# A chunked state-space scan before a squared-ReLU feed-forward layer: 64-token chunks on 32x32 array tiles

## The chip, the cores and the metric

The kernel runs on one core of a Trainium2 chip. A core has five engines with queues of their own: TensorE (PE; its weight loads are shown as PEld), VectorE (DVE), ScalarE (ACT), GpSimd (POOL) and SyncE (SP, here only a DMA queue). The metric is the device time of one execution in microseconds, and lower is better. A profile is of one execution; its clock starts at its first instruction.

## The reference

Inputs are x (4 x 8 x 768 x 32), a (4 x 8 x 768), B and C (4 x 8 x 768 x 16) and the two weights of the feed-forward layer, w_in (256 x 2048) and w_out (2048 x 256). Cut to what matters, and with the batch and the head left out:

```python
log_a = np.log(np.clip(a, 1e-06, 1.0))
for c in range(S // 32):                       # chunks of 32 tokens
    cum = np.cumsum(log_a[sl])
    L = np.exp(cum[:, None] - cum[None, :]) * causal
    y[sl] = ((Cc @ Bc.T) * L) @ xc + (Cc @ state) * np.exp(cum)[:, None]
    state = np.exp(cum[-1]) * state + (Bc * np.exp(cum[-1] - cum)[:, None]).T @ xc
out = np.maximum(y_all @ w_in, 0) ** 2 @ w_out     # y_all: 3072 tokens x 256 (8 heads x 32)
```

The size of the chunk doesn't change the result: a longer one moves work from the state to the product inside the chunk. N = 16 is the size of a state, D = 32 that of a head.

## The kernel before

The 3072 tokens are cut into 12 blocks of 256 (a batch and a third of its sequence; `PAIRS`, L107). Each block goes through the scan, which yields T, and then through the feed-forward layer in eight pairs of 128-wide slices.

The feed-forward layer sets the beat. There are 96 steps (L385), one for each block and pair of slices. In step s, `mm1` (L296) issues four 128x128 products with 256 columns into a PSUM tile hps (two buffers), ACT applies the ReLU (L305), DVE squares the result of the step before (L311), and `mm2` (L314) issues four products of the step `LAG` = 4 earlier into ops. After a block's last slice ACT copies ops to osb (L326), and SP stores it (L327).

Between these, the scan of a coming block is issued in small parts. A block is two chunks (u) of 128 tokens, each with 64 even and 64 odd tokens (r). For block k, with s0 = 8k - 12, the dictionary `todo` of the loop at L405 holds:

- s0 - 12: `ph_load` of C, B and x on SP (L118);
- s0 - 4: `ph_prep` on POOL: C times the running product of a into cz (L142), B cast into Bb (L156), x divided by the running product into xs (L162);
- s0: `ph_tr`, six transposes on TensorE (L181, L183) into PSUM, and DVE's copy to bct (L185);
- s0 + 1: `ph_u`, 16 products of B and x (L224, array tiles of 64 rows x 32 columns), and DVE's state updates (L237 to L241);
- s0 + 2: `ph_mt`, 16 products of B and C with 256 columns (L195, tiles of 32 x 64), then four masks on DVE (L206);
- s0 + 6: `ph_y`, 16 products with the state (L264, tiles of 32 x 32 on the diagonal) and 32 with the masked matrix (L276, tiles of 64 x 32), and ACT's copy to T (L290).

All four share one PSUM tile of four banks (`ps_s`, tag A), one after the other. Each engine runs its instructions in the order written (`manual_schedule`), and semaphores hold an instruction until what it reads is written and what it writes is free. Blocks 0 and 1 are scanned ahead of the loop. The weights come in five pairs of DMAs, the first pair on ACT's queue and the rest on SP's, between the loads of blocks 0 to 3; ACT casts w_in (L133) and POOL w_out (L134).

Of the kernel before, what the change touches and what calls it, by code (L numbers as in the profile page):

```python
# [10 lines left out]
FP32 = mybir.dt.float32  # L11
BF16 = mybir.dt.bfloat16
# [18 lines left out]
def kernel(  # L31
# [16 lines left out]
    NPAIR = 12  # L48
    LAG = 4
    LEAD = 12  # L50
# [6 lines left out]
    big = ctx.enter_context(tc.tile_pool(name="big", bufs=2))  # L57
# [10 lines left out]
    tok = 2 * np.arange(64)[None, :] + np.arange(2)[:, None]  # L68
    later = tok.reshape(-1)
    mask_np = np.zeros((128, 2, 128), np.float32)  # L70
    for u in range(2):
        for r in range(2):
            mask_np[64 * u:64 * u + 64, r, :] = (tok[r][:, None] <= later[None, :])
# [6 lines left out]
    cb_np = np.concatenate([np.eye(128, dtype=np.float32), mask_np.reshape(128, 256)],  # L80
                           axis=1).astype(ml_dtypes.bfloat16)
# [18 lines left out]
    cz = [const.tile([128, 2, 240], BF16, name=f"cz{i}") for i in range(3)]  # L100
# [6 lines left out]
    PAIRS = [(b, j) for j in range(3) for b in range(4)]  # L107


    loaded = {}  # L110

    def ph_load(k, order="CBx", eng=None):
        b, j = PAIRS[k]
        t = {}
        for what in order:
            src, w = {"B": (B, N), "C": (C, N), "x": (x, D)}[what]
            dst = nat.tile([128, NH, 2 * w], FP32, tag=f"{what}_nat", name=f"{what}_nat{k}")
            (eng or nc.sync).dma_start(  # L118
                out=dst, in_=_dap(src, (b * NH * S + j * 256) * w,
                                  [[2 * w, 128], [S * w, NH], [1, 2 * w]]))  # L120
            t[what] = dst
        loaded[k] = t
# [13 lines left out]

    live = {}

    def prep_c(k, eng):
        b, j = PAIRS[k]  # L140
        czk = cz[k % 3]
        eng.tensor_tensor(  # L142
            out=_fap(czk, 0, [[240, 2], [32, 8], [1, 16]]),
            in0=_fap(loaded[k]["C"], 0, [[16, 2], [32, 8], [1, 16]]),
            in1=_fap(P_sb, b * 24 + j, [[96, 2], [3, 8], [0, 16]]), op=ALU.mult)
        live.setdefault(k, {})["cz"] = czk

    def prep_b(k, eng):
        Bb = prep.tile([128, 2, 128], BF16, tag="Bb", name=f"Bb{k}")
        for r in range(2):  # L150
            bo = _fap(Bb, r * 128, [[16, 2], [32, 4], [1, 16]])
            bi = _fap(loaded[k]["B"], r * 16, [[128, 2], [32, 4], [1, 16]])
            if eng is nc.scalar:
                eng.copy(out=bo, in_=bi)  # L154
            else:
                eng.tensor_copy(out=bo, in_=bi)  # L156
        live.setdefault(k, {})["Bb"] = Bb

    def prep_x(k, eng):
        b, j = PAIRS[k]  # L160
# [7 lines left out]
    def ph_prep(k):  # L168
        prep_c(k, nc.gpsimd)
        prep_b(k, nc.gpsimd)  # L170
        prep_x(k, nc.gpsimd)
# [3 lines left out]
    def ph_tr(k):  # L175
        v = live[k]
        pool, tag = (ps_o, "ops") if k < 2 else (ps_s, "A")
        tr = pool.tile([128, 2, 3, 128], BF16, tag=tag, name=f"tr{k}",
                       padded_shape=[128, 2, 4, 128] if k < 2 else [128, 8, 4, 128])
        for r in range(2):  # L180
            nc.tensor.transpose(tr[:, r, 0, :], v["Bb"][:, r, :], eye_b)  # L181
            for g in range(2):
                nc.tensor.transpose(tr[:, r, 1 + g, :], v["cz"][:, r, 112 * g:112 * g + 128], eye_b)  # L183
        bct = big.tile([128, 2, 3, 128], BF16, tag="bct", name=f"bct{k}")
        nc.vector.tensor_copy(out=bct, in_=tr)  # L185
        v["bct"] = bct

    def ph_mt(k):
        v = live[k]
        bct = v["bct"]  # L190
        mt = ps_s.tile([128, 4, 2, 2, 128], FP32, tag="A", name=f"mt{k}")
        for u in range(2):
            for r in range(2):
                for q in range(4):
                    nc.tensor.matmul(  # L195
                        mt[64 * u:64 * u + 64, q, r, :, :],
                        bct[32 * q:32 * q + 32, r, 0, u * 64:u * 64 + 64],
                        _fap(bct[32 * q:32 * q + 32], 128 + u * 64, [[128, 2], [384, 2], [1, 64]]),
                        start=True, stop=True, skip_group_check=True,
                        tile_position=(32 * q, 64 * u))  # L200
        v["mt"] = mt
        v["mts"] = big.tile([128, 4, 2, 2, 128], BF16, tag="mts", name=f"mts{k}")

    def ph_mask(k, q):
        v = live[k]
        nc.vector.tensor_tensor(  # L206
            out=v["mts"][:, q], in0=v["mt"][:, q],
            in1=_fap(cb, 128, [[128, 2], [0, 2], [1, 128]]), op=ALU.mult)

    def ph_u(k):  # L210
        b, j = PAIRS[k]
        v = live[k]
        if k < 2:
            U = [ps_h.tile([128, 64], FP32, tag="hps", name=f"U{k}_{u}", padded_shape=[128, 512])
                 for u in range(2)]
        else:
            t = ps_s.tile([128, 4, 512], FP32, tag="A", name=f"U{k}")
            U = [t[:, u, 0:64] for u in range(2)]
        for r in range(2):
            for u in range(2):  # L220
                if j == 2 and u == 1:
                    continue
                for q in range(4):
                    nc.tensor.matmul(  # L224
                        U[u][32 * q:32 * q + 32, :],
                        v["Bb"][64 * u:64 * u + 64, r, 32 * q:32 * q + 32],
                        _fap(v["xs"][64 * u:64 * u + 64], r * 256 + q * 32, [[128, 2], [1, 32]]),
                        start=(r == 0), stop=(r == 1), skip_group_check=True,
                        tile_position=(64 * u, 32 * q))
        S_u = [state.get(b)]  # L230
        for u in range(2):
            if j == 2 and u == 1:
                break
            ptot = Ptot[:, u, b * 3 + j:b * 3 + j + 1]
            S_n = spool.tile([128, 64], BF16, tag=f"S{b}{u}", name=f"S{k}_{u}")
            if S_u[u] is None:
                nc.vector.tensor_scalar(out=S_n, in0=U[u], scalar1=ptot, scalar2=None, op0=ALU.mult)  # L237
            else:
                z = spool.tile([128, 64], FP32, tag="z", name=f"z{k}_{u}")
                nc.vector.tensor_tensor(out=z, in0=U[u], in1=S_u[u], op=ALU.add)  # L240
                nc.vector.tensor_scalar(out=S_n, in0=z, scalar1=ptot, scalar2=None, op0=ALU.mult)  # L241
            S_u.append(S_n)
        v["S"] = S_u
        state[b] = S_u[-1]
# [3 lines left out]
    def ph_y(k):  # L248
        b, j = PAIRS[k]
        v = live.pop(k)  # L250
        if k < 2:
            Y = [ps_h.tile([128, 2, 128], FP32, tag="hps", name=f"Y{k}_{u}", padded_shape=[128, 4, 128])
                 for u in range(2)]
        else:
            t = ps_s.tile([128, 4, 4, 128], FP32, tag="A", name=f"Y{k}")
            Y = [t[:, u, 0:2, :] for u in range(2)]
        first = {(u, q): True for u in range(2) for q in range(4)}
        for u in range(2):
            S_b = v["S"][u]
            if S_b is None:  # L260
                continue
            for g in range(2):
                for q in range(4):
                    nc.tensor.matmul(  # L264
                        Y[u][32 * q:32 * q + 32, g, :],
                        S_b[32 * q:32 * q + 32, g * 32:(g + 1) * 32],
                        _fap(v["bct"][32 * q:32 * q + 32], 128 + g * 128 + u * 64, [[384, 2], [1, 64]]),
                        start=first[(u, q)], stop=False, skip_group_check=True,
                        tile_position=(32 * q, 32 * q))
                    first[(u, q)] = False  # L270
        for g in range(2):
            for r in range(2):
                for u in range(2):
                    for q in range(4):
                        h = 4 * g + q
                        nc.tensor.matmul(  # L276
                            Y[u][32 * q:32 * q + 32, g, :],
                            v["xs"][64 * u:64 * u + 64, r, h * 32:h * 32 + 32],
                            v["mts"][64 * u:64 * u + 64, q, r, g, :],
                            start=first[(u, q)], stop=(g == 1 and r == 1), skip_group_check=True,  # L280
                            tile_position=(64 * u, 32 * q))
                        first[(u, q)] = False

# [160 lines left out]
```

## Time and profile before

| what | value |
|---|---|
| median of 3 runs | 131.57 us (131.39 to 131.71) |
| span of the profiled execution | 129.5 us |
| own time of the profiled execution | the page gives none beside the span; 2.0 us lie between it and the median |
| busy: TensorE, DVE, ACT, POOL | 86%, 70%, 58%, 24% |
| mean granted TensorE clock | 0.997 |
| large products mm1, mm2 (L301, L321) | 384 each, mean 277 and 273 ns |
| ReLU (L305), square (L311), mask (L206) | 599, 500 and 685 ns |
| cz, Bb, xs on POOL (L142, L156, L162) | 682, 319 and 1126 ns |
| loads of C, B, x: issue to landing | 3.5, 4.1, 4.2 us |
| store of the output: issue to landing | 2.2 us |

In a line of groups stand the line of the code, the engine, the operation, what it writes and reads with shapes, the count, the busy time, the mean of one, and the idle time before it with what ended that. A matmul's length holds its way through the array, so matmuls overlap and their starts tell the pace. In the chain and in the timeline the columns are the start in us, the length in us, and what ran. "SPq" is time in SP's queue, "issue" an idle time that nothing shown by the profile ended.

### The profile page before, as it was taken

To read this page: it belongs to the slowest core of one execution; us is meant where nothing else is said; L and a number is where in the kernel's file an instruction comes from. 1 tells how busy PE (TensorE), PEld (TensorE's weight loads), DVE (VectorE), ACT (ScalarE), POOL (GpSimd) and SP (SyncE) were. 2 spreads that over 40 slices of the span, in tenths; PEclk is the share of its full clock that TensorE was granted. 3 is DMA by queue.
4 is the path that set the end of the run, shared out by engine and by line. 5 is a ranking of instruction groups with operands and counts; after the bars stand their busy time and mean duration, and the time that the engine had idled before them with its cause. 6 is when DMAs were issued, how large, how long until landed. Compare 5 with 4: busy or idle time off the path is not lost.

```text
span 129.5 us, 4148 instructions
## 1 busy us (share of the span) xinstructions
PE 111.8 (86%) x1740; PEld 87.8 (68%) x1740; DVE 90.4 (70%) x201; ACT 75.7 (58%) x134; POOL 31.6 (24%) x54
## 2 busy tenths in 40 slices
PE   0126648699999999999999999999999999999980
PEld 0013315557877787788778777887887787788860
DVE  0519592379899698795896995886977938744520
ACT  0413308867757657658467476576584675687740
POOL 4015236335907025060070240330330000000000
PEclk9999999999999999999999999999999999999998
DMA  4999999978391280650831903805602010020202
GB/s 95 257 165 262 294 175 269 318 148 154 96 200 21 88 161 6 137 106 5 177 69 47 196 10 96 149 3 135 116 0 89 3 68 18 0 86 0 81 0 81
DMA packets 43043, 14.18 MB, mean 110 GB/s; under 512 B 37840, under 2 KB 40720, under 8 KB 43024
## 3 DMA queue, kind: packets, MB, share of 16 engines
q1 hardware_dynamic: 42224, 13.21, 43.8%
q10 hardware_dynamic: 800, 0.71, 1.8%
q8 instruction: 13, 0.21, 0.7%
q14 instruction: 6, 0.05, 0.1%
HBM read 10.77 MB, written 3.15 MB: 107 GB/s over the span
## 4 chain that ended last, share of the span: by engine, by line
PE 76%; SPq 11%; DMA 8%; ACT 1%; issue 1%
PE ops L321 34%; PE hps L301 30%; SPq L118 8%; DMA w_in_f<-in_moe_w_in_dram 6%; PE mt L195 3%; PE Y L276 3%; PE Y L264 2%; DMA cf<-const_f 2%; SPq L125 2%; PE tr L183 2%; PE U L224 1%; SPq L128 1%; ACT w_in_b L133 1%; PE tr L181 1%; ACT osb L326 0%
## 5 line engine op out<-in xcount | busy, mean ns | idle before, releaser
L305 ACT ACTIVATE hb<-hps 128x512 bf16<-128x512 f32 x96 | 57.5, 599 | 32.2 <-PE hps L301 31.1
L301 PE MATMUL hps<-T,w_in_b 128*128 128x256 bf16 x384 | 58.5, 277 | 1.8 <-ACT w_in_b L133 1.4
L321 PE MATMUL ops<-w_out_b,h 128*128 128x256 bf16 x384 | 57.3, 273 | 0.0
L311 DVE TENSOR_TENSOR h<-hb 128x512 bf16<-128x512 bf16 x96 | 45.9, 500 | 9.4 <-ACT hb L305 9.4
L301 PEld LDWEIGHTS <-w_in_b 128*128 128x128 bf16 x384 | 38.0, 99 | 7.6 <-ACT w_in_b L133 1.9
L321 PEld LDWEIGHTS <-h 128*128 128x128 bf16 x384 | 34.7, 98 | 7.0 <-issue 2.0
L206 DVE TENSOR_TENSOR mts<-mt,cb 128x512 bf16<-128x512 f32 x48 | 31.5, 685 | 2.8 <-PE mt L195 2.7
L162 POOL TENSOR_TENSOR xs<-x_nat,Pinv 128x512 bf16<-128x512 f32 x12 | 13.5, 1126 | 15.0 <-DMA x_nat<-in_x_dram 11.7
L142 POOL TENSOR_TENSOR cz<-C_nat,P_sb 128x256 bf16<-128x256 f32 x10 | 6.8, 682 | 40.4 <-DMA C_nat<-in_C_dram 28.8
L185 DVE COPY bct<-tr 128x768 bf16<-128x768 bf16 x12 | 6.7, 556 | 13.4 <-PE tr L183 13.4
L326 ACT COPY osb<-ops 128x512 f32<-128x512 f32 x12 | 7.0, 580 | 1.6 <-PE ops L321 1.6
L276 PE MATMUL Y<-mts,xs 64*32 64x128 bf16 x384 | 6.2, 232 | 1.8 <-DVE mts L206 1.8
L181 PE MATMUL tr<-cb,Bb 128*128 128x128 bf16 x24 | 5.1, 232 | 3.0 <-ACT Bb L154 3.0
L290 ACT CAST T<-Y 128x512 bf16<-128x512 f32 x10 | 5.9, 586 | 1.3
L195 PE MATMUL mt<-bct 32*64 32x256 bf16 x192 | 5.7, 302 | 0.7 <-DVE bct L185 0.7
L156 POOL CAST Bb<-B_nat 128x128 bf16<-128x128 f32 x20 | 5.8, 319 | 1.8 <-DMA B_nat<-in_B_dram 1.7
L264 PE MATMUL Y<-bct,S 32*32 32x128 bf16 x160 | 4.6, 225 | 1.9 <-DVE S L237 1.9
L276 PEld LDWEIGHTS <-xs 64*32 64x32 bf16 x384 | 3.4, 95 | 3.8 <-issue 1.7
L183 PE MATMUL tr<-cb,cz 128*128 128x128 bf16 x48 | 5.9, 235 | 0.0
L134 POOL CAST w_out_b<-w_out_f 128x1024 bf16<-128x1024 f32 (+1 forms) x5 | 4.3, 868 | 6.0 <-DMA w_out_f<-in_moe_w_out_dram 6.0
L264 PEld LDWEIGHTS <-S 32*32 32x32 bf16 x160 | 2.3, 91 | 4.3 <-DVE S L237 2.2
L287 ACT CAST T<-Y 128x256 bf16<-128x256 f32 x4 | 1.3, 376 | 6.5 <-PE Y L276 6.5
(29 smaller groups left out, 37.8 us busy)
## 6 DMA issues: line engine op xcount, KB each, us to landing
x_nat<-in_x_dram SPq DMA_DIRECT2D x12, 256.0 KB, 4.2
out_dram<-osb SPq DMA_DIRECT2D x12, 256.0 KB, 2.2
C_nat<-in_C_dram SPq DMA_DIRECT2D x12, 128.0 KB, 3.5
B_nat<-in_B_dram SPq DMA_DIRECT2D x12, 128.0 KB, 4.1
w_in_f<-in_moe_w_in_dram SPq DMA_DIRECT2D x3, 512.0 KB, 5.8
w_out_f<-in_moe_w_out_dram SPq DMA_DIRECT2D x3, 512.0 KB, 7.1
w_in_f<-in_moe_w_in_dram ACTq DMA_DIRECT2D x1, 256.0 KB, 4.8
w_out_f<-in_moe_w_out_dram ACTq DMA_DIRECT2D x1, 256.0 KB, 5.2
```

The source lines that it names most:

```text
L118: (eng or nc.sync).dma_start(out=dst, in_=_dap(src, (b * NH * S + j * 256) * w, [[2 * w, 128], [S * w, NH], [1, 2 * w]]))
L162: eng.tensor_tensor(out=_fap(xs, 0, [[256, 2], [32, 8], [1, 32]]), in0=_fap(loaded[k]["x"], 0, [[32, 2], [64, 8], [1, 32]]), in1=_fap(Pinv ...
L183: nc.tensor.transpose(tr[:, r, 1 + g, :], v["cz"][:, r, 112 * g:112 * g + 128], eye_b)
L195: nc.tensor.matmul(mt[64 * u:64 * u + 64, q, r, :, :], bct[32 * q:32 * q + 32, r, 0, u * 64:u * 64 + 64], _fap(bct[32 * q:32 * q + 32], 12 ...
L206: nc.vector.tensor_tensor(out=v["mts"][:, q], in0=v["mt"][:, q], in1=_fap(cb, 128, [[128, 2], [0, 2], [1, 128]]), op=ALU.mult)
L264: nc.tensor.matmul(Y[u][32 * q:32 * q + 32, g, :], S_b[32 * q:32 * q + 32, g * 32:(g + 1) * 32], _fap(v["bct"][32 * q:32 * q + 32], 128 + ...
L276: nc.tensor.matmul(Y[u][32 * q:32 * q + 32, g, :], v["xs"][64 * u:64 * u + 64, r, h * 32:h * 32 + 32], v["mts"][64 * u:64 * u + 64, q, r, ...
L301: nc.tensor.matmul(hps[:, i, :], w_in_b[:, g, f * 128:(f + 1) * 128], T[blk][:, g].rearrange("p r u t -> p (r u t)"), start=(g == 0), stop ...
L305: nc.scalar.activation(out=hb, in_=hps, func=AF.Relu)
L311: nc.vector.tensor_tensor(out=h2, in0=hb, in1=hb, op=ALU.mult)
L321: nc.tensor.matmul(ops[blk][:, r, :], h2[:, i, r * 128:(r + 1) * 128], w_out_b[:, f, :], start=(f == 0 and r == 0), stop=(f == 15), skip_g ...
L326: nc.scalar.copy(out=osb, in_=ops.pop(blk).rearrange("p r d -> p (r d)"))
```

## The change

A block is now four chunks (c) of 64 tokens, each with 32 even and 32 odd ones; chunk c lies on partitions 32c to 32c + 31 of x and B. The products of the scan use 32 x 32 tiles of the array, 16 positions.

- `small` takes the place of `ph_u`, `ph_mt` and `ph_y`. It issues in one run the y of block k and the u and m of block k + 1: at most 4 products of the full array with the state (128 x 128, block-diagonal over the heads), 64 of 32 x 32 with 64 columns, 64 with 32 columns, and 32 with 128 columns. In the loop it stands at step 8k - 2. Its PSUM tile `sp` is allocated once; in each of its four banks m has columns 0 to 255, y 256 to 383 and u 384 to 511.
- The masks are two operations of 512 columns a block in place of four.
- The state is [128, 128], with a block of 32 x 32 for each quarter of the partitions. `ph_s` updates it in four operations on DVE, one a chunk, and POOL makes a product `left` at even chunks that DVE reads at odd ones. The scale Ptot is applied once for two chunks.
- The operands of the transposes are made by POOL in a tile `jt` (C in two operations, B in two), and a second copy of B in `bz` (one more cast).
- From block `NPE` = 4 on, `ph_tr` is a DMA transpose of jt into bct on SP's queue, at step 8k - 17. Blocks 0 to 3 stay on TensorE; blocks 2 and 3 at step 8k - 12.
- `ph_load` stands at 8k - 28 and `ph_prep` at 8k - 20. Before, they stood at 8k - 24 and 8k - 16.
- Only block 0's y is ahead of the loop; block 1's y comes in the loop at step 6. Some memsets move from POOL to DVE, and the tiles bct and mts have three buffers in place of two.

The diff, cut to its core:

```diff
-    LEAD = 12
+    NPE = 4
...
-    big = ctx.enter_context(tc.tile_pool(name="big", bufs=2))
+    big = ctx.enter_context(tc.tile_pool(name="big", bufs=3))
...
-    cz = [const.tile([128, 2, 240], BF16, name=f"cz{i}") for i in range(3)]
+    jt = [const.tile([128, 2, 3, 128], BF16, name=f"jt{i}") for i in range(3)]
+    bz = [const.tile([128, 2, 240], BF16, name=f"bz{i}") for i in range(3)]
...
+    sp = ps_s.tile([128, 4, 512], FP32, name="sp")
...
+        for g in range(2):
+            eng.tensor_tensor(
+                out=_fap(jt[k % 3], 128 + 144 * g, [[384, 2], [32, 4], [1, 16]]),
+                in0=_fap(loaded[k]["C"], 128 * g, [[16, 2], [32, 4], [1, 16]]),
+                in1=_fap(P_sb, b * 24 + 12 * g + j, [[96, 2], [3, 4], [0, 16]]), op=ALU.mult)
...
+    def prep_bz(k, eng):
+        cast(eng, _fap(bz[k % 3], 0, [[240, 2], [32, 8], [1, 16]]),
+             _fap(loaded[k]["B"], 0, [[16, 2], [32, 8], [1, 16]]))
...
     def ph_tr(k):
+        v = live.setdefault(k, {})
+        bct = big.tile([128, 2, 3, 128], BF16, tag="bct", name=f"bct{k}")
+        v["bct"] = bct
+        if k >= NPE:
+            nc.sync.dma_start_transpose(out=bct.rearrange("p r w t -> p (r w) t"),
+                                        in_=jt[k % 3].rearrange("p r w t -> p (r w t)"))
+            return
+        pool, tag = (ps_o, "ops") if k < 2 else (ps_h, "hps")
+        tr = pool.tile([128, 2, 3, 128], BF16, tag=tag, name=f"tr{k}", padded_shape=[128, 2, 4, 128])
+        for r in range(2):
+            for w in range(3):
+                nc.tensor.transpose(tr[:, r, w, :], jt[k % 3][:, r, w, :], eye_b)
+        nc.vector.tensor_copy(out=bct, in_=tr)
...
+    def small(y=None, m=None, u=None):
+        begun = set()
+        def mm(bank, quads, dst, w, v, pos):
+            need = [(bank, q) for q in quads if (bank, q) not in begun]
+            assert len(need) in (0, len(quads))
+            begun.update(need)
+            nc.tensor.matmul(dst, w, v, start=bool(need), stop=False, skip_group_check=True,
+                             **({} if pos is None else {"tile_position": pos}))
+        if y is not None:
+            vy = live[y]
+            for c in range(4):
+                S_c = vy["S"][c]
+                if S_c is None:
+                    continue
+                mm(c, range(4), sp[:, c, 256:384], S_c,
+                   _fap(vy["bct"], 128 + 32 * c, [[128, 2], [384, 2], [1, 32]]), None)
+            for g in range(2):
+                for r in range(2):
+                    for c in range(4):
+                        for q in range(4):
+                            mm(c, [q], sp[32 * q:32 * q + 32, c, 256 + 64 * g:320 + 64 * g],
+                               vy["xs"][32 * c:32 * c + 32, r, (4 * g + q) * 32:(4 * g + q) * 32 + 32],
+                               vy["mts"][32 * c:32 * c + 32, q, r * 128 + g * 64:r * 128 + g * 64 + 64],
+                               (32 * c, 32 * q))
+        if u is not None:
...
+            for g in range(2):
+                for r in range(2):
+                    for c in range(4 - last):
+                        for q in range(4):
+                            mm(c, [q], sp[32 * q:32 * q + 32, c, 384 + 32 * q:416 + 32 * q],
...
+                               (32 * c, 32 * q))
+        if m is not None:
...
+            for r in range(2):
+                for c in range(4):
+                    for q in range(4):
+                        mm(q, [c], sp[32 * c:32 * c + 32, q, r * 128:r * 128 + 128],
...
+                           (32 * q, 32 * c))
+        if y is not None:
+            T[y] = tpool.tile([128, 2, 2, 128], BF16, tag="T", name=f"T{y}")
+            nc.scalar.copy(out=_fap(T[y], 0, [[32, 4], [128, 4], [1, 32]]),
+                           in_=_fap(sp, 256, [[512, 4], [32, 4], [1, 32]]))
+            live.pop(y)
...
+    def ph_mask(k, q0, q1):
+        nc.vector.tensor_tensor(
+            out=live[k]["mts"][:, q0:q1], in0=sp[:, q0:q1, 0:256],
+            in1=_fap(cb, 128, [[0, q1 - q0], [1, 256]]), op=ALU.mult)
...
+    def ph_s(k, c):
...
+        if c % 2 == 0:
+            if prev is None:
+                nc.vector.tensor_copy(out=S_n, in_=U)
+            else:
+                nc.vector.tensor_tensor(out=S_n, in0=U, in1=prev, op=ALU.add)
+            if not (j == 2 and c == 2):
+                v["left"] = spool.tile([128, 128], FP32, tag="left", name=f"left{k}_{c}")
+                nc.gpsimd.tensor_scalar(out=v["left"], in0=S_n, scalar1=ptot, scalar2=None, op0=ALU.mult)
+        else:
+            nc.vector.scalar_tensor_tensor(out=S_n, in0=U, scalar=ptot, in1=v["left"],
+                                           op0=ALU.mult, op1=ALU.add)
...
+        for k in range(1, NU):
+            s0 = 8 * k - 2
+            if k + 1 < NU:
+                at(s0, small, y=k, m=k + 1, u=k + 1)
+                for i in range(2):
+                    at(s0 + 1 + i, ph_mask, k + 1, 2 * i, 2 * i + 2)
+                at(s0 + 3, ph_s, k + 1, 0)
+                at(s0 + 4, ph_s, k + 1, 1)
+                at(s0 + 4, ph_s, k + 1, 2)
+                at(s0 + 5, ph_s, k + 1, 3)
+            else:
+                at(s0, small, y=k)
+        for k in range(2, NU):
+            if k >= 4:
+                at(8 * k - 28, ph_load, k)
+            if k >= 3:
+                at(8 * k - 20, ph_prep, k)
+            at(8 * k - (12 if k < NPE else 17), ph_tr, k)
```

Ahead of the loop, unit 0's m and u, its masks and its four state updates now come before unit 1's preparation on DVE and POOL, and unit 1's m and u before the first mm1.

## The prediction

> **What bounds the kernel now.** I read the page's busy shares first, then its chain, then the groups of TensorE, and last the timeline of one steady block.
>
> ```profile
> PE 111.8 (86%) x1740; PEld 87.8 (68%) x1740; DVE 90.4 (70%) x201; ACT 75.7 (58%) x134; POOL 31.6 (24%) x54
> ...
> PE 76%; SPq 11%; DMA 8%; ACT 1%; issue 1%
> ```
>
> TensorE (PE) is busiest, and the chain that ended last lies on it for 76%. The other 19% are SP and DMA, and they lie at the start, as the chain in order of time shows:
>
> ```profile
> 18.81 7.32 DMA w_in_f<-in_moe_w_in_dram
> 26.15 1.05 ACT w_in_b L133
> 27.25 0.61 PE hps L301 x4
> ...
> 123.65 2.20 PE ops L321 x20
> 125.87 0.59 ACT osb L326
> ```
>
> So there are two stages. Until 27.25 us the last quarter of w_in is late: step 6 waits for it. From 27.25 to 125.85 us the chain is TensorE alone, and only TensorE's own time in this second stage moves the end. In it one block lasts 8.90 us (the stretches 57.2 to 66.1 and 66.1 to 75.0 repeat it). The timeline of TensorE over one block (start, length, line):
>
> ```profile
> 57.68 0.60 PE L301 MATMUL hps<-T,w_in_b 128*128 128x256 bf16 x4
> 58.21 0.40 PE L264 MATMUL Y<-bct,S 32*32 32x128 bf16 x16
> 58.54 0.42 PE L276 MATMUL Y<-mts,xs 64*32 64x128 bf16 x32
> 58.89 0.61 PE L321 MATMUL ops<-w_out_b,h 128*128 128x256 bf16 x4
> 59.34 0.60 PE L301 MATMUL hps<-T,w_in_b 128*128 128x256 bf16 x4
> ...
> 60.65 0.22 PE L181 MATMUL tr<-cb,Bb 128*128 128x128 bf16 x1
> ...
> 60.98 0.60 PE L321 MATMUL ops<-w_out_b,h 128*128 128x256 bf16 x4
> 61.42 0.60 PE L301 MATMUL hps<-T,w_in_b 128*128 128x256 bf16 x4
> 61.95 0.25 PE L224 MATMUL U<-xs,Bb 64*32 64x64 bf16 x16
> 62.14 0.61 PE L321 MATMUL ops<-w_out_b,h 128*128 128x256 bf16 x4
> 62.58 0.60 PE L301 MATMUL hps<-T,w_in_b 128*128 128x256 bf16 x4
> 63.14 0.44 PE L195 MATMUL mt<-bct 32*64 32x256 bf16 x16
> 63.51 0.61 PE L321 MATMUL ops<-w_out_b,h 128*128 128x256 bf16 x4
> ```
>
> Read the starts, not the lengths. Four large products take 0.437 us (109 ns each). Subtracting that, the small work costs: Y 58.12 to 58.89 = 0.77; transposes 60.65 to 60.98 = 0.33 (55 ns each); U 61.86 to 62.14 = 0.28; mt 63.02 to 63.51 = 0.49. Together 1.87 us, and 16 x 0.437 + 1.87 = 8.86, the block. Much of it is no streaming: between the due end of one array shape and the first start of the next lie 0.09 us (58.12 to 58.21, 61.86 to 61.95), and the same again on the way out. A block changes shape seven times (Y three, U two, mt two), about 0.63 us.
>
> Inside a group the pace is that of issue: U's 16 weight loads (mean 91 ns) span 0.14 us, so one pair of load and matmul starts each (0.14 - 0.09)/15 = 3.4 ns. A pass over tiles with 128 columns takes 56 ns by its starts.
>
> **What the Trainium skill says.** "TensorEngine Tiling (Array Packing)", Key Properties: changing the tiling mode drains the engine. The trace agrees, with 0.09 us. "TensorE: Matmul & The Clock Gate", Part 3: tiles that don't conflict start about 4 ns apart; the trace has 3.4, but with at most 8 tiles at work, never 16. The same page's table of specifications gives TensorE a queue of 64; no view here shows its depth. "VectorE: DVE Perf Modes", The three transpose paths: a 128x128 bf16 DMA transpose takes 1309 ns; "DMA: Bandwidth & Descriptors", Latency and other measured facts: 261 GB/s for DMA transposes. No run here shows either.
>
> **The change part by part,** on TensorE after 27.25 us.
>
> Removed: of unit 2, mt and Y (0.49 + 0.77; its transposes and U come before 27.25), and units 3 to 11 whole, 9 x 1.87 = 16.8. Sum 18.1 us.
>
> Added: one burst a block (y of k, u and m of k+1) of 4 full-array products and 160 small ones.
> - Inter product, 4 of 128 weight columns at the transposes' 55 ns: 0.22. It needs no change of shape before it.
> - One change of shape: 0.09.
> - 64 + 64 + 32 pairs on 16 tiles. A pass of 16 pairs at 3.4 ns takes 54 ns to issue; streaming asks 56 ns at 128 columns and less at 64 or 32. So issue sets it: 160 x 3.4 = 0.545.
> - The last stream, 53 ns, and the change back, 0.09.
>
> A burst is 1.0 us. Ten come after step 6 (units 2 to 11 as k+1), 10.0 us; block 11's y alone 0.65; unit 3's transposes, still on TensorE, 0.33. Sum 11.0, gain 18.1 - 11.0 = 7.1 us. TensorE instructions per block grow from 300 (150 pairs) to 456.
>
> Beside TensorE, per block of then about 8.0 us:
> - DVE: masks halve (2 x 0.69 in place of 4), the copy of tr (0.56) goes from unit 4, four state operations of 128 columns at 0.25 to 0.3 take the place of four of 64 at 0.22 to 0.28. About 6.4 us with 8 squares at 0.5; hidden.
> - ACT: as before, 8 x 0.60 + 0.59 + 0.58 = 6.0; hidden. T is copied at step 8k-2 and used at 8k: two steps, 1.7 us less the burst's tail, against 0.2 + 0.59. Covered by 0.9 us; if it failed, mm1 would wait the rest each block.
> - POOL: two products of half size (0.35), two casts (0.32), the cast of bz (0.6, by the 256-element cz row at 0.68), xs 1.13, two "left" products of 128 (0.3 to 0.4): 3.9 us. New: S at odd chunks waits on DVE for POOL, with the squares queued behind it. mm2 uses a square three steps later (2.6 us); a POOL round trip of 0.5 to 1.2 us fits. If POOL sits in xs(3), whose input landed at 31.74, DVE stalls about 2 us once; I charge 0.5 us.
> - SP: each transpose (196 KB) is queued behind the output and the three loads, which take 2.4 us to issue (61.08 to 63.48), and waits there for POOL's jt; behind it wait the next output and loads, needed a block later. It issues near step 8k-18 and is needed at 8k-10 plus 0.85 us of burst: 7.8 us. Cost from both sides: 196 KB at 261 GB/s is 0.75, plus the 2.2 us that an output takes to land: 3 us; serial, 6 x 1.31 + 2.2 = 10 us. Below nothing it can't be, as nothing that ends earlier than the need moves the burst. I take 4 to 5 us (loads of like size land in 3.5 to 4.2), hidden.
> - Instruction fetch: queue 8 moved 13 packets, 0.21 MB, for 3480 TensorE instructions, so 16 KB is about 260 instructions, and took 0.7% of 16 engines' 129.5 us, 1.1 us each. A burst of 324 can cross two such blocks. I charge 0.4 us, range 0 to 3.
>
> The start: no weight DMA moves in its queue, so step 6 still starts near 27.25. TensorE, DVE and POOL reach the first mm1 by 17.5 to 19 us by my count (20.11 before) although unit 0's S chain now stands ahead of unit 1's preparation; four steps take 3.2 us, so some 4 us of cover. A later start costs nothing until it is used up, then one for one.
>
> Sum: 7.1 - 0.5 - 0.4 = 6.2 us off. The profiled span is 129.5, and 2.0 us lie around it up to the median of 131.57. I count against the span, 129.5 - 6.2 = 123.3, and leave the 2.0 as they are: 125.3, rounded up to 125.4.
>
> **The rivals.**
>
> Supply of instructions. The burst is 324 instructions, and the kernel before never issues more than 96 in a row. Those 96 start within 0.54 us (67.11 to 67.65); if 64 stood in the queue, 32 came in meanwhile, so supply is proved only to 17 ns per instruction. Below, issue at 1.7. With r per instruction a burst is 260 r + 0.1: break-even at (18.1 - 1.0)/10 = 1.7 us, r = 6.2 ns. For it: nothing in the profile is that dense for that long. Against: 300 instructions a block come without one stall, and after the 96 the next large products run at 109 ns at once. At the geometric middle of 3.4 and 17, 7.6 ns, a burst is 2.1 us: 18.1 - 22.0 = 3.9 us slower, 135.5. This is the case on the other side.
>
> Transposes late. At 10 us each of 8 bursts waits 10 - 7.8 = 2.2 us, less what the sum gained: 125.4 + 17.6 = 143. Decides from 7.8 us. Against: loads of like size land in half that.
>
> Part of the gain lost to the POOL to DVE round trip, fetch, or supply at 4 to 6 ns: about half, 128.5.
>
> That the change doesn't do what it says: the built program has the bursts in one run and no transposes on TensorE from unit 4, so I give this nothing.
>
> **Chances.** Forecast 0.50 (123 to 127); part lost 0.13 (127 to 131); supply 0.24, of which 0.12 lies above 138; late transposes 0.10, most above 138; no change 0.03. Supply and transposes both end slower: 0.34. A difference of about 0.2% is all that a measurement of this kernel can tell from none. Leaving out the upper half of the supply case and some of the late one, the range is 123 to 138; the likeliest case's own is 123 to 127.
>
> **What would show it.** Right: the burst's sp group starts and the next ops product starts 1.0 us apart, block period 8.0 us, no TensorE wait on DMA bct, step 6 still at 27 us. Supply: 160 pairs spread over 1.5 us or more with no releaser but issue. Transposes: bct landing over 7.8 us after issue and TensorE waiting for it. I would be wrong too if 16 tiles do not run side by side as 8 do.

## The result, and the profile after

| | before | after |
|---|---|---|
| median of the runs | 131.64 us (131.39 to 132.51, 4 runs) | 145.16 us (143.97 to 147.07, 4 runs) |
| ratio after / before, 95% interval | | 1.098 (1.090 to 1.106) |
| profiled execution: time, span | 131.57, 129.5 us | 144.76, 143.0 us |
| mean granted TensorE clock | 0.997 | 0.964 |

The change makes the kernel 9.8% slower; the forecast was 125.4 us. The slowest of the four runs after is left out of the ratio.

The page of the changed kernel, its busy shares and its chain by engine (the same lines as those shown of before):

```profile
PE 116.1 (81%) x2696; PEld 98.5 (69%) x2696; DVE 77.1 (54%) x182; ACT 76.3 (53%) x134; POOL 53.6 (37%) x95
...
PEclk9999999595599999999999999999999999999999
...
q8 instruction: 21, 0.34, 1.1%
...
PE 77%; issue 7%; DMA 5%; POOL 4%; DVE 3%; SPq 1%; ACT 0%; POOLq 0%; DVEq 0%
```

TensorE has 2696 matmuls in place of 1740 and is busy 4.3 us longer. "issue" is now 7% of the chain, where it was 1%: TensorE stood still and no semaphore that the profile shows held it. PEclk shows a half clock in the slices from 25 to 28.6 and from 32 to 39 us. Queue 8, which carries instructions, moved 21 packets where it moved 13.

The chain of the changed kernel in order of time (start, length, what):

```profile
28.87 1.62 PE sp L204 x161
30.49 3.07 issue
...
48.05 0.74 issue
...
53.55 1.64 PE sp L204 x162
...
72.64 1.77 issue
...
84.37 1.70 issue
...
112.62 1.07 issue
```

Two things differ from the forecast. A burst that runs through takes 1.64 us in the chain, and the large group behind it 0.1 us longer than others; the forecast had 1.0 for both. And five times TensorE stops for 0.74 to 3.07 us, twice inside a burst, three times behind one.

One burst without a pause, in the timeline of TensorE (start, length, line, operation, count):

```profile
52.95 0.60 PE L290 MATMUL hps<-T,w_in_b 128*128 128x256 bf16 x4
53.39 0.33 PE L204 MATMUL sp<-bct,S 128*128 128x128 bf16 x3
53.65 0.68 PE L204 MATMUL sp<-mts,xs 32*32 32x64 bf16 x64
54.14 0.73 PE L204 MATMUL sp<-xs,bz 32*32 32x32 bf16 x64
54.70 0.49 PE L204 MATMUL sp<-bct 32*32 32x128 bf16 x32
55.13 0.61 PE L310 MATMUL ops<-w_out_b,h 128*128 128x256 bf16 x4
```

From 53.39 to 55.13 the small work takes 1.74 us; that is what the prediction counted as 1.0. The 64 pairs with 64 columns take 0.49 us by the starts, the 64 with 32 columns 0.56: the time does not follow the columns. By the single starts in the trace, the first 32 pairs of a burst come 3.3 to 4.0 ns apart; then TensorE stops for 0.11 to 0.13 us; all later pairs come 8.3 ns apart, in all three shapes (34 ns where the kind changes). In this burst that is 0.12 + 0.11 + 1.10 = 1.33 us from the first pair to the last. With 0.26 from the first inter product to the first pair and 0.14 on the way out it is the 1.74. The prediction had 160 x 3.4 = 0.545 in place of the 1.33.

Two of the pauses, the first and the fourth, in the same timeline:

```profile
30.02 0.47 PE L204 MATMUL sp<-bct 32*32 32x128 bf16 x31
33.56 0.28 PE L204 MATMUL sp<-bct 32*32 32x128 bf16 x1 [3.07 <-issue]
...
83.88 0.49 PE L290 MATMUL hps<-T,w_in_b 128*128 128x256 bf16 x3
86.07 0.28 PE L290 MATMUL hps<-T,w_in_b 128*128 128x256 bf16 x1 [1.70 <-issue]
```

At 33.56 one pair is cut off a group of 32, at 86.07 one product off a group of four that has nothing to do with the change. What they share is their number in TensorE's records (weight loads and matmuls, counted from the start). The packets of queue 8, set beside it:

```
TensorE record   last start   gap to the next   packet of 16 KB ends   TensorE goes on
 958 = 256x4-66    30.27          3.29 us             32.22                33.56
1470 = 256x6-66    47.78          1.01                47.36                48.79
2750 = 256x11-66   72.42          1.99                73.06                74.41
3262 = 256x13-66   84.10          1.97                84.73                86.07
4542 = 256x18-66  112.35          1.34                112.24               113.69
```

Each pause stands at a multiple of 256 records less 66, and each ends 1.34 to 1.45 us after a 16-KB packet of instructions has landed (0.34 MB in 21 packets is 16 KB each). In the kernel before, TensorE reached each such boundary at least 5.5 us after the packet's end, and never paused.

Where the 13.5 us of span went, counted from step 6 (large products: 185 groups of four at 0.437 us, 80.9 us in both):

| term | before | after | difference |
|---|---|---|---|
| start of step 6 | 27.25 | 27.98 | +0.7 |
| small work without pauses (what is left of the stretch) | 17.7 | 18.2 | +0.5 |
| five pauses, gaps less what the records need there anyway | 0 | 9.3 | +9.3 |
| large products on the half clock | 0 | 2.9 | +2.9 |

The sum is 13.4. The half clock behind the first pause by itself, in the table by stretches (stretch, length, busy time and count of PE, PEld, DVE, ACT and POOL, granted clock, DMA share, GB/s):

```profile
33.80:38.90 5.10, 5.10 (x26) 3.53 (x26) 3.08 (x8) 1.78 (x3) 0.60 (x1) 0.51 0.02 4
39.30:43.70 4.40, 4.38 (x44) 3.81 (x42) 2.52 (x7) 3.13 (x6) 3.50 (x7) 1.00 0.19 61
```

For 5.1 us behind the longest pause, 26 matmuls were done at a clock of 0.51, where the next 4.4 us did 44 at 1.00.

### The profile page after: what moved, and what is told of

Same layout as the page of the kernel before. It is cut to its first block, busy times and chain, and to the rows that moved or that the text cites. A ratio compares the mean times of both kernels' runs of the same rounds, so it can differ in the third digit from the quotient of the medians.

```text
span 143.0 us, 6092 instructions
## 1 busy us (share of the span) xinstructions
PE 116.1 (81%) x2696; PEld 98.5 (69%) x2696; DVE 77.1 (54%) x182; ACT 76.3 (53%) x134; POOL 53.6 (37%) x95
## 4 chain that ended last, share of the span: by engine, by line
PE 77%; issue 7%; DMA 5%; POOL 4%; DVE 3%; SPq 1%; ACT 0%; POOLq 0%; DVEq 0%
PE ops L310 32%; PE hps L290 30%; PE sp L204 15%; DMA x_nat<-in_x_dram 5%; DVE mts L252 2%; POOL left L275 2%; PE tr L191 1%; DVE S L277 1%; POOL xs L165 1%; SPq L119 1%; POOL jt L151 1%; POOL jt L142 1%; DVE S L272 0%; ACT osb L315 0%; POOL w_out_b L135 0%
## 5 line engine op out<-in xcount | busy, mean ns | idle before, releaser
L275 POOL TENSOR_SCALAR left<-S,Ptot 128x128 f32<-128x128 bf16 x20 | 12.4, 622 | 64.4 <-DVE S L272 47.3
L252 DVE TENSOR_TENSOR mts<-sp,cb 128x512 bf16<-128x512 f32 x24 | 16.3, 688 | 26.8 <-ACT T L247 24.6
L247 ACT CAST T<-sp 128x512 bf16<-128x512 f32 x12 | 7.0, 586 | 21.1 <-PE sp L204 21.1
L277 DVE SCALAR_TENSOR_TENSOR S<-sp,Ptot,left 128x128 bf16<-128x128 f32 x20 | 7.0, 350 | 9.2 <-POOL left L275 9.2
L142 POOL TENSOR_TENSOR jt<-C_nat,P_sb 128x128 bf16<-128x128 f32 x20 | 9.2, 477 | 0.0
L204 PE MATMUL sp<-xs,bz 32*32 32x32 bf16 x704 | 8.3, 186 | 1.0 <-POOL xs L165 0.9
L151 POOL CAST jt<-B_nat 128x128 bf16<-128x128 f32 x20 | 8.2, 438 | 0.0
L204 PE MATMUL sp<-mts,xs 32*32 32x64 bf16 x768 | 8.2, 199 | 0.0
L204 PEld LDWEIGHTS <-bz 32*32 32x32 bf16 x704 | 7.1, 89 | 1.6 <-issue 1.3
L204 PEld LDWEIGHTS <-xs 32*32 32x32 bf16 x768 | 6.6, 88 | 1.6 <-issue 0.2
```

Source lines behind the costliest of these rows:

```text
L142: eng.tensor_tensor(out=_fap(jt[k % 3], 128 + 144 * g, [[384, 2], [32, 4], [1, 16]]), in0=_fap(loaded[k]["C"], 128 * g, [[16, 2], [32, 4], ...
L151: eng.tensor_copy(out=out, in_=in_)
L204: nc.tensor.matmul(dst, w, v, start=bool(need), stop=False, skip_group_check=True, **({} if pos is None else {"tile_position": pos}))
L247: nc.scalar.copy(out=_fap(T[y], 0, [[32, 4], [128, 4], [1, 32]]), in_=_fap(sp, 256, [[512, 4], [32, 4], [1, 32]]))
L252: nc.vector.tensor_tensor(out=live[k]["mts"][:, q0:q1], in0=sp[:, q0:q1, 0:256], in1=_fap(cb, 128, [[0, q1 - q0], [1, 256]]), op=ALU.mult)
L275: nc.gpsimd.tensor_scalar(out=v["left"], in0=S_n, scalar1=ptot, scalar2=None, op0=ALU.mult)
```

## The experiments

Theory F (fetch): TensorE holds two blocks of 256 instructions; when it has run through one, the next is fetched, and it can go on in it some 4.6 us after it had only 64 instructions of the one before left. The 4.6 was fitted to the five pauses; with the times of the trace it gives 3.1, 0.8, 1.2, 2.4 and 1.5 us for the 3.3, 1.0, 2.0, 2.0 and 1.3 measured. The rivals go by these letters in the expectations: the DMA transposes or another transfer hold TensorE (T); it waits for other engines or full buffers, in certain blocks of the work (W); the 16-tile form is dear in itself, wherever it stands (B); the pace of decoding alone explains a dense run (D).

**72 idle instruction pairs, early.** If records decide, the pauses move to other work.

```diff
+        pad = ps_o.tile([128, 512], FP32, tag="ops", name="pad")
+        for i in range(72):
+            q = i % 4
+            nc.tensor.matmul(pad[32 * q:32 * q + 32, 0:32], cb[0:32, 0:32], cb[0:32, 0:32],
+                             start=True, stop=True, skip_group_check=True, tile_position=(0, 32 * q))
```

> The changed kernel with 72 idle pairs of weight load and matmul (32x32, a few ns each) put on TensorE early in the start, at about 7 us. Nothing else moves; the stream is 144 instructions longer, so every later burst lies elsewhere against the blocks of 256 instructions. Theory F (fetch): TensorE's instructions come in 16 KB blocks of 256, two at a time, and a new block is there about 4.6 us after 64 instructions were left of the one before; TensorE pauses when 256 are used up sooner. Worked on the changed kernel's own starts, the five pauses at 30, 48, 72, 84 and 112 us (9.3 us in all) go, and three come near 51, 62 and 101 us, of about 1.1, 2.4 and 0.9 us, 4.4 in all; the pause of 3.3 us in the first burst goes, and with it the slow clock behind it (2.4 us). Time 138.5 (136.5 to 140.5). Theory T (the DMA transposes or another transfer hold TensorE up) and theory W (waits on other engines): the pauses stay where they are, 145 plus or minus 1.

Measured 141.94 us (141.55 to 144.48) beside 132.46 of before, ratio 1.072 (1.065 to 1.079). With 144 records more, in front of the steady stage, the kernel is faster than the changed one. Its timeline at the two longest late pauses:

```profile
48.64 0.31 PE L204 MATMUL sp<-bct 32*32 32x128 bf16 x11
50.40 0.30 PE L204 MATMUL sp<-bct 32*32 32x128 bf16 x21 [1.46 <-issue]
...
59.87 0.49 PE L290 MATMUL hps<-T,w_in_b 128*128 128x256 bf16 x3
62.88 0.28 PE L290 MATMUL hps<-T,w_in_b 128*128 128x256 bf16 x1 [2.52 <-issue]
```

and its chain, in which the first burst now runs through:

```profile
29.50 1.64 PE sp L204 x162
...
101.77 0.73 issue
...
117.17 0.71 issue
```

The pauses stand at records 1982, 2494 and 4286, again 256n - 66, within 2.3 us of the three places foretold; two more of 0.5 to 0.9 us by the starts (at 3774 and 5054) were not foretold. The same work runs through in one place and stops in another, which T and W had not foretold. The total lies above the range of 136.5 to 140.5, since I had left out that the pause at 60 us would bring a half clock (63.5 to 66.6 us) of its own.

**The burst in three parts, two steps apart (y, then m, then u).** If 324 instructions in one run outpace the fetch, smaller groups do not.

```diff
-                at(s0, small, y=k, m=k + 1, u=k + 1)
+                at(s0, small, y=k)
+                at(s0 + 2, small, m=k + 1)
+                at(s0 + 4, small, u=k + 1)
```

Masks and state updates move two steps later with it.

> The changed kernel with y, m and u issued at three places two steps apart instead of in one run; the same instructions. Theory F: no 256 instructions are used up in under about 4.2 us any more, so the pauses fall from 9.3 to under 1.5 us in all and the slow clock after the first goes; each part starts with 64 instructions waiting, at 1.7 ns, and two more changes of array shape cost 0.18 us each, which nearly cancel (a block's small work 1.75 us for 1.64). Time 133 (131.5 to 135.5). Theory B (the pairs on 16 tiles are dear in themselves, wherever they stand): 145 plus 1, as two more changes of shape come to each block.

Measured 138.0 us (137.85 to 138.02), ratio 1.043 (1.038 to 1.048). No pause at a block boundary is left in the steady stage, and that took 7 us off, so B, which had foretold 146, falls as the cause of the pauses. It stayed above its range because the late u makes the state late, a new wait. Its timeline at one of five such places:

```profile
46.79 0.27 PE L290 MATMUL hps<-T,w_in_b 128*128 128x256 bf16 x1
47.53 0.33 PE L204 MATMUL sp<-bct,S 128*128 128x128 bf16 x3 [0.47 <-DVE S L277]
```

From one start to the next are 0.74 us where 0.1 is due: five times some 0.65, about 3.3 us in all.

**The transposes of all blocks on TensorE (NPE = 12).** If DMA transposes or their queue stop TensorE, the pauses go; if records do, they stay.

```diff
-    NPE = 4
+    NPE = 12
```

> The changed kernel with all transposes on TensorE (NPE = 12): no DMA transpose. Theory T (DMA transposes hold up the instruction blocks or the loads): the pauses go, 145.2 - 9.3 - 2.4 + 8 x 0.33 = 136. Theory F: pauses stay, as the bursts stay; 12 more instructions a block shift them to the boundaries before records 958, 1470, 2750, 3262, 3774 and 5054, 8.5 us in all (5 to 10), and the time is 145.2 + 2.6 - 0.8 = 147 (144 to 149).

Measured 150.18 us (149.31 to 151.9), ratio 1.133 (1.124 to 1.142). No DMA transposes are left, but the chain has the pauses:

```profile
30.71 3.31 issue
...
48.77 0.49 issue
...
74.42 1.12 issue
...
85.18 1.75 issue
...
126.95 1.14 issue
```

By single starts they stand at records 958, 1470, 2750, 3262, 3774 and 5054, the six that were foretold. T falls. The time is 3 us above the expectation and above its range; a second stretch of half clock, 87.8 to 90.5 us behind the pause at 85, and a step 6 that starts 0.5 us later are part of it.

**The disputed cost by itself.** 768 idle pairs of 32 columns on 16 tiles, appended to the kernel before; this adds work that nothing uses.

```diff
+        run = ps_s.tile([128, 4, 512], FP32, tag="A", name="run")
+        for i in range(768):
+            c, q = (i // 4) % 4, i % 4
+            nc.tensor.matmul(run[32 * q:32 * q + 32, c, 0:32], w_in_b[32 * c:32 * c + 32, 0, 0:32],
+                             w_out_b[32 * c:32 * c + 32, 0, 0:32], start=True, stop=True,
+                             skip_group_check=True, tile_position=(32 * c, 32 * q))
```

> The kernel before with 768 pairs of 32x32 (32 columns, 16 tiles, four banks, results unused) appended after its last product: 1536 instructions without any wait, which adds work that the reference has not. Theory F: 1536 are six blocks of 256; each is used up in about 1.1 us (1.7 ns for the first 64, then about 4.2 ns an instruction) and TensorE then pauses until the next block, so the run takes 6 x 3.5 to 4.6 = 21 to 28 us, with pauses of 2.5 to 3.5 us every 256 records. Theory D (decoding alone sets the pace): 1536 x 4.2 ns = 6.4 us without pauses.

A single execution took 148.82 us, span 147.0. The timeline of its appended run:

```profile
127.68 1.34 PE L417 MATMUL run<-w_out_b,w_in_b 32*32 32x32 bf16 x147
130.41 1.19 PE L417 MATMUL run<-w_out_b,w_in_b 32*32 32x32 bf16 x128 [1.38 <-issue]
134.14 1.23 PE L417 MATMUL run<-w_out_b,w_in_b 32*32 32x32 bf16 x128 [2.54 <-issue]
138.14 1.22 PE L417 MATMUL run<-w_out_b,w_in_b 32*32 32x32 bf16 x128 [2.78 <-issue]
141.59 1.22 PE L417 MATMUL run<-w_out_b,w_in_b 32*32 32x32 bf16 x128 [2.23 <-issue]
145.05 1.06 PE L417 MATMUL run<-w_out_b,w_in_b 32*32 32x32 bf16 x109 [2.23 <-issue]
```

This is the cleanest view of the cause. There is no DVE, ACT or SP work to wait for, and still TensorE does 128 pairs (256 instructions) in about 1.1 us, 8.3 ns a pair behind the first 32, and then waits over 2 us for the next 256. A block comes every 3.45 to 4.0 us. Other transfers do not set that time, as the DMA share from 130.4 us on is 0.02 to 0.04. From 132.5 us on the granted clock is 0.50 and the pairs still come 8.3 ns apart, so the array's clock does not set their pace. The run took 18.4 us, a little under F's 21 to 28, because the first 147 pairs were there when it began; the rival's 6.4 is far off.

**The three parts again, with u ahead of m**, so that the state is early as in the changed kernel.

```diff
-                at(s0 + 2, small, m=k + 1)
-                at(s0 + 4, small, u=k + 1)
+                at(s0 + 2, small, u=k + 1)
+                at(s0 + 4, small, m=k + 1)
```

The state updates go back to where the changed kernel has them, the masks move two steps on.

> The split kernel with u second and m third (y, u, m two steps apart), so that the state operations keep their old steps and only the masks move, to one and two steps before the next y. The split kernel's five waits of 0.74 us on the state should go. Theory F: no pauses, 138.0 - 3.3 = 134.7 (133.5 to 135.7); what is left over the kernel before is that a block's small work on TensorE takes about 2.0 us in three runs of 32x32 pairs against 1.87. Rival: the masks come late now and y waits for them in place of the state: 138.

Measured 136.53 us (135.7 to 137.92) beside 132.13, ratio 1.033 (1.022 to 1.045), span 134.1, clock 0.998. The waits on the state are gone, one pause of 0.46 us is left, at record 2750, and no half clock follows. The time is still above the range of 133.5 to 135.7: in the profiled executions, 138.02 and 135.92 us, 2.7 of the 3.3 us went from step 6 on, but step 6 started 0.6 us later. One steady block of its timeline:

```profile
56.22 0.39 PE L204 MATMUL sp<-bct,S 128*128 128x128 bf16 x4
56.53 0.68 PE L204 MATMUL sp<-mts,xs 32*32 32x64 bf16 x64
57.15 0.61 PE L310 MATMUL ops<-w_out_b,h 128*128 128x256 bf16 x4
...
59.00 0.65 PE L204 MATMUL sp<-xs,bz 32*32 32x32 bf16 x64
59.58 0.61 PE L310 MATMUL ops<-w_out_b,h 128*128 128x256 bf16 x4
...
61.43 0.33 PE L204 MATMUL sp<-bct 32*32 32x128 bf16 x32
61.70 0.61 PE L310 MATMUL ops<-w_out_b,h 128*128 128x256 bf16 x4
```

From the end of the large products before each, that is 0.93 (56.22 to 57.15), 0.68 and 0.36 us: 1.97 a block, against 1.87 of the kernel before with its transposes. So this form, pauses apart, does not pay: it has 160 pairs for what 80 pairs did. Against the changed kernel it is 8.6 us faster, which is what pauses and half clock cost (12.2) less 2.7 of dearer small work (20.9 from step 6 on, by the same reckoning), the pause that is left, and a step 6 that starts 0.3 later.

**The transposes alone moved to DMA, in the kernel before.**

```diff
+        if k >= NPE:
+            nc.sync.dma_start_transpose(out=bct.rearrange("p r w t -> p (r w) t"),
+                                        in_=jt[k % 3].rearrange("p r w t -> p (r w t)"))
+            return
...
-                at(s0 - 12, ph_load, k)
+                at(s0 - 16, ph_load, k)
...
-                at(s0 - 4, ph_prep, k)
-            at(s0, ph_tr, k)
+                at(s0 - 8, ph_prep, k)
+            at(s0 if k < NPE else s0 - 5, ph_tr, k)
```

> The kernel before with one part of the change alone: from block 4 on the transposes are DMA transposes of a tile jt (loads and preparation four steps earlier, the transpose five steps before the place of the old one). 128-token chunks, tiles and places of the products as before. If a DMA transpose is hidden, eight blocks lose 0.33 us of TensorE each: 2.6 us, ratio 0.980 (128.5 to 130). Rival: the transposes come late, or delay the loads behind them on the queue, and TensorE waits for bct: 132 or more.

Measured 129.16 us (128.65 to 130.01), ratio 0.980 (0.971 to 0.989): faster than both kernels, as expected; whether by as much as 2% the interval leaves open. From step 6 on the profiled execution is 2.2 us shorter than that of the kernel before, where the expectation had 2.6.

**And u joined to y in the 64-row form**, two changes of shape less a block, 64 pairs in a row and not 160.

```diff
+        if k + 1 in joined:
+            ph_u(k + 1, t)
...
-            at(s0 + 1, ph_u, k)
+            if k not in joined:
+                at(s0 + 1, ph_u, k)
```

> As the last, and from block 4 on the 16 products U of the next block directly behind the products Y, in the same array shape (64 x 32) and in two free banks of Y's tile: the change's idea of one place, kept to a run of 64 pairs. Two changes of shape a block go (0.18 us and the tail of a stream), and U's 32 instructions come at 4.2 ns in place of 1.7 (0.08 us dearer): 8 x 0.15 = 1.2 us less than the last one, ratio 0.971 (127 to 129). 128 instructions in a run leave the fetch of instructions far from its limit. Rival: the saved changes of shape are eaten by waits on the state or on xs: no better than the last one.

Measured 128.26 us (127.85 to 129.26), ratio 0.974 (0.963 to 0.985). Its timeline where the two are joined:

```profile
57.26 0.60 PE L308 MATMUL hps<-T,w_in_b 128*128 128x256 bf16 x4
57.79 0.40 PE L269 MATMUL Y<-bct,S 32*32 32x128 bf16 x16
58.12 0.42 PE L281 MATMUL Y<-mts,xs 64*32 64x128 bf16 x32
58.38 0.32 PE L228 MATMUL Y<-xs,jt 64*32 64x64 bf16 x16
58.63 0.61 PE L328 MATMUL ops<-w_out_b,h 128*128 128x256 bf16 x4
```

The large products are due to end at 57.26 + 0.437 = 57.70, so Y and U together take 0.93 us, where they took 0.77 + 0.28 = 1.05 in the kernel before. Over eight blocks the 0.12 make 1.0 us, about the 0.9 that this version is faster than the one above. It is the fastest version tried. That the 0.9 is real is likely, not shown: the two intervals overlap.

## Why the prediction was wrong

Right were the frame and the covers:

- Two stages with the seam at step 6: it started at 27.98, and TensorE reached the first large product at 18.75, in the 17.5 to 19 that were given. The late 0.7 us is the last quarter of w_in, which landed at 26.85 us and not at 26.13: ACT's cast of it ended at 27.92 (27.20 before), and step 6 started 0.05 us behind it in both kernels. A half clock from 25.2 us on, which slowed the large products ahead of step 6, would by itself have held it only to 27.8.
- DMA transposes hidden. The estimate was 4 to 5 us from issue to landing, and the DMA view of the changed kernel has

```profile
bct<-jt SPq DMA_TRANSPOSE x8, 5.0
```

No wait of TensorE on bct is in the trace.
- DVE, ACT and POOL hidden. POOL's "left" products take 622 ns where 0.3 to 0.4 us was assumed, and DVE waits 9.2 us in all for them, but TensorE does not wait for DVE in the steady stage.
- The change of shape at 0.09 us, the masks at 0.69 us and the large products at 0.437 us for four stood.

Two steps failed.

"So issue sets it: 160 x 3.4 = 0.545." The 3.4 ns came from U, a group of 16 pairs. Only the first 32 pairs of a burst keep that pace; the others come at 8.3 ns, 4.2 ns an instruction, behind a stop of 0.11 us. 32 pairs are 64 instructions, the depth of the queue that the prediction cited, so that these stood in the queue is a likely reason. It is not shown: in the dense run the first 32 pairs behind each pause come 3.9 ns apart too, where TensorE had just been idle for over 2 us. The ten bursts take 1.62 to 1.85 us each, pauses taken off (four of them have 144 pairs, not 160). All small work is 18.2 us, where the sum had 11.0 and 17.7 was removed. This alone takes the gain away and makes hardly a loss.

The supply rival had the right side, and its price was worked wrongly. "A burst is 260 r + 0.1" leaves out the inter product, the two changes of shape and the last stream, 0.45 us that the forecast's own burst of 1.0 contains. With them and the 0.1 the break-even of 1.7 us lies at (1.7 - 0.55) / 260 = 4.4 ns an instruction, not at 6.2, and the measured 4.2 is close to it. The middle of 7.6 ns is that of 3.4 ns a pair and 17 ns an instruction, two different things. (A smaller slip: the 7.8 us that a transpose has are counted from step 8k - 17, where the code issues it, and not from 8k - 18.)

"Instruction fetch: ... A burst of 324 can cross two such blocks. I charge 0.4 us, range 0 to 3." It cost 9.3 us, and the half clock behind it, which no step had, 2.9. I had priced the packet's own time, 1.1 us. What counts is how long after the last boundary the next block can be run: 4.6 us in the theory that fits the five pauses, 3.45 to 4.0 in the dense run. With 456 instructions in a block of 8.7 us the mean supply is enough (8.7 / 456 x 256 = 4.9 us for a block of instructions); with 324 of them in 1.64 us it is not, whenever a boundary falls into a burst shortly after another. The kernel before has 300 in 8.9 us, with at most 96 in a row, and crosses boundaries 6.7 to 8.7 us apart.

Together, against the 123.3 of span that were forecast: 7.2 for the bursts and the other small work added, 0.4 for small work removed, 9.3 - 0.4 for the fetch, 2.9 for the half clock, 0.7 for the later step 6, and 0.5 less as DVE's stall did not come. That is 19.6 of the 19.7 us.

The Trainium skill has this in a page that the prediction did not use: "Runtime: NRT & Kernel Launch", Instruction fetch mechanics. It says that instructions come in blocks of 16 KiB, 256 instructions, into two lines, and this case's trace agrees (16 KB a packet, and pauses only at one place in every 256 records). It adds that crossing a boundary is "mostly hidden", because instructions are dispatched more slowly than they are fetched. Here the measurement decides: small matmuls went at 1.7 to 4.2 ns an instruction, a fetched block at 3.45 to 4.0 us / 256 = 13 to 16 ns, and the fetch was not hidden.

What stays open: which part of a fetch (the request, the packet, what follows its landing) makes up the time; the runs show only that TensorE goes on 1.28 to 1.64 us after the packet's end, over all pauses of 0.46 us and more from 27 us on that stand at a block boundary. And when a pause brings the half clock. "TensorE: Matmul & The Clock Gate", Part 1, says that the clock drops after an idle window of about 3.4 us. The traces agree in the length: in each run the granted clock changes only at times that lie whole multiples of 3.41 us apart. But a drop did not need an idle window. In the changed kernel the clock was at half from 32.0 us on, when TensorE had been idle for 1.7 us. Before the drops behind pauses in other runs (two with all transposes on TensorE, one with the idle pairs early, one in the dense run) the window held 2.5, 2.0, 2.8 and 2.4 us of pause. The pause of 2.0 us at 84.10 in the changed kernel, whole in one window, brought no drop. Where 1.7 and 2.0 us were enough, small products took part of the window; in the one at 84.10 the rest was large products but for the last of a burst. Whether that decides, no run tests.

## What to carry to other kernels

Count TensorE's instructions in each stretch and not only their streaming time: splitting products into smaller tiles doubles the count, and beyond the first 64 in a row a pair of load and matmul on 32x32 tiles took 8.3 ns with 32, 64 and 128 columns alike. Where 256 instructions would start in less than the 3.45 to 4.0 us that a fetched block took in the dense run, let the small groups stand apart between large products; gathering them saves changes of shape at 0.09 us each and can cost 1 to 3 us at a time. An idle TensorE whose releaser is "issue" at record numbers 256 apart is a wait for instructions, and the test for it is to shift the count, not to move the work.

## What the runs showed of the hardware

- TensorE started instructions 1.7 to 2.0 ns apart for the first 64 of a burst, stopped for 0.11 to 0.13 us, and went on at 4.2 ns an instruction; that later pace was the same for 32, 64 and 128 columns on 32x32 tiles, and with 32 columns at clocks of 1.00 and 0.50.
- A dense run of such pairs gets 256 instructions per 3.45 to 4.0 us, and is idle for some two thirds of it.
- After a pause of 3.3 us the large products took 213 ns in place of 109 for about 5 us.
- A DMA transpose of 196 KB from SBUF to SBUF landed a median 5.0 us after its issue in the changed kernel and 3.7 us in the kernel before with its transposes moved, well under the 10 us that six serial transposes were reckoned to take.
